# Order of the DMA transposes and of the loads of batches 3 and 4 in an attention and GEGLU kernel

## The chip, the cores and the metric

The kernel runs on one core of a Trainium2 chip. The metric is the device time of one execution in microseconds; of several runs the median is given. Beside it stands the profile of one execution: what each engine (TensorE or PE, VectorE or DVE, ScalarE or ACT, GpSimd or POOL, SyncE or SP) did, and what the DMA queues moved.

## The reference

Two steps follow each other: causal sliding-window attention with a linear bias by distance, for 8 batches, 8 heads, 576 positions and 64 dimensions per head, and then a gated feed-forward layer on its 4608 output rows of 512.

```python
scores = scale * np.matmul(q, k.transpose(0, 1, 3, 2))
rel = pos[:, None] - pos[None, :]
mask = (rel >= 0) & (rel < 128)
scores = np.where(mask, scores - slopes[h] * np.abs(rel), -1e9)
attn = softmax(scores)                       # over the keys
x = np.matmul(attn, v)                       # (8, 8, 576, 64) -> (4608, 512)
out = (gelu(x @ w_gate) * (x @ w_val)) @ w_out   # 512 -> 1536 -> 512
```

## The kernel before

Everything is scheduled by hand: the program text gives each engine's order of instructions, and each engine works through its own list.

**Two granularities run against each other.** The feed-forward part works on nine groups g of 512 tokens, the attention on eight batches b of 576 positions. The outer loop is over the groups. In group g, `gate_val` (L648 are its matmuls) makes the twelve hidden tiles `hT`, and then the products with `w_out` follow. Between these products the attention of the batches ahead is done: in group g the scores of batch b = g + 2, and the products of probabilities and values (`values`, matmuls at L502) of batch b - 1. From group 2 on, `out_products` does the output with seven block products instead of eight: `P(n, a)` is product n of half a, six matmuls at L749, and `O(what, a)` takes a result out of PSUM. Some of the factors are sums of blocks, kept in `left` (by group) and `right` (once).

**What the scores need.** `scores2(b, c)` (L301) multiplies transposed q with transposed k, two heads' pairs at a time. The transposes are made by DMA: `load_qk(b)` and `load_v(b)` request q, k and v from DRAM through POOL's queue (five requests each, line L115, with a cast from float32 to bfloat16) into `qs`, `ks` and `vb`, and `transposes_dma(b)` issues on SP's queue five transposes of q (L185, `qT<-qs`) and one large transpose of k (L178, `kT<-ks`). All five tensors have two buffers, taken by b % 2: batch 4 uses the buffers that batch 2 had.

**What sets the order on the queues.** SP's list holds the transposes, the stores of the output (`store`, L675) and short instructions that relay a matmul's end (L212). POOL's list holds the requests; a `tensor_copy` of two elements into `mark` is a way to wait: POOL reads one element of a tile and so stands until that tile has been written, and the requests behind it stand too. Group 1 has three such marks: on `ks[1]` (L1131, batch 3's k has been loaded), on `qT[1]` (L1132, its q has been transposed) and on `kT[1]` (L1134, its k has been transposed). v of batch 3 is requested behind the first two, q and k of batch 4 behind the third. In groups 2 to 5 a mark on a hidden tile (L1164) comes ahead of the next requests. `transposes_dma(g + 2)` is called at the top of group g, so the transposes of batch 4 are in SP's list ahead of all that group 2 stores.

**The softmax denominators.** From batch 3 on, `sums4` makes the row sums in the gate stage, `gather` (L451) writes their reciprocals to DRAM on ScalarE's queue and `spread_dma` (L457, `rb<-rd`) reads them back to all partitions, two transfers of 576 KB.

Of the kernel before, what the change touches and what calls it, by code (L numbers as in the profile page):

```python
# [34 lines left out]
def kernel(  # L35
# [10 lines left out]
    nc = tc.nc  # L46
# [27 lines left out]
    def keep_busy(ps, n, w=64, rhs=None):  # L74
        for _ in range(n):
# [21 lines left out]
    mark = consts.tile([1, 2], BF16, name="mark")  # L97

    qs, ks = ([consts.tile([128, 5, DM], BF16, name=f"{nm}s{i}") for i in range(2)]
              for nm in "qk")  # L100
    qT, kT = ([consts.tile([128, 4, 640], BF16, name=f"{nm}T{i}") for i in range(2)]
              for nm in "qk")
# [8 lines left out]
    def load(t, src, b, js=range(5), last=0):  # L111
        for j in js:
            n = rows(j)
            at = last if j == 4 else 0
            nc.gpsimd.dma_start(  # L115
                out=t[at:at + n, j, :].rearrange("p (h d) -> p h d", h=H),
                in_=src[b][:, 128 * j:128 * j + n, :].rearrange("h p d -> p h d"))

    def load_qk(b):
        load(qs[b % 2], q, b)  # L120
        load(ks[b % 2], k, b)

    def load_v(b, js=range(5)):
        load(vb[b % 2], v, b, js, 64)
# [44 lines left out]
    def transpose(b, what, c, copy):  # L169
        ps = bank().bitcast(BF16)  # L170
        for n, lo in ((0, 0), (1, 384)):
            transpose_runs(b, n, what, c, ps[:, lo:576])
        for n, lo in ((0, 0), (1, 384)):
            untangle(copy, b, n, what, c, c + 1, ps[:, lo:576])

    def transposes_dma(b):
        def of_k():
            nc.sync.dma_start_transpose(  # L178
                out=kT[b % 2].rearrange("p c (j t) -> p (c j) t", t=128),
                in_=ks[b % 2].rearrange("p j x -> p (j x)"))  # L180

        if b > 3:
            of_k()
        for j in range(5):
            nc.sync.dma_start_transpose(  # L185
                out=qT[b % 2][:, :, 128 * j:128 * j + 128], in_=qs[b % 2][:, j, :])
        if b <= 3:
            of_k()


# [482 lines left out]
    def store():  # L673
        for args in stores:
            nc.sync.dma_start(**args)  # L675
        stores.clear()
# [128 lines left out]
    for h in (0, 2, 4, 6):  # L805
        for w, src in ((0, q), (1, k)):
            (nc.scalar if w and h == 0 else nc.sync).dma_start(
                out=raw[w][h // 4].rearrange("p (h x) -> p h x", h=4)[:, h % 4:h % 4 + 2, :],
                in_=src[0][h:h + 2, 0:384, :].rearrange("h (p r) d -> p h (r d)", r=3))
# [115 lines left out]
    for do in inverse_a:  # L925
        do[1]()
    dve(out=pairs1.rearrange("p x (h d) -> p h x d", d=64),
        in_=vb[1].rearrange("p j x -> p (j x)")[:, 0:1536].rearrange(
            "p (h x d) -> p h x d", h=H, x=3))
# [46 lines left out]
    for n in range(4):  # L976
        nc.gpsimd.dma_start(
            out=wo[:, 3 * n:3 * n + 3, :],
            in_=moe_w_out[384 * n:384 * n + 384, :].rearrange("(c p) f -> p c f", p=128))
# [28 lines left out]
    def exp_table():  # L1008
        nc.scalar.preload_act_table_set("natural_log_exp_and_others")
# [4 lines left out]
    def out_products(g):  # L1014
        b = g + 2
        O = lambda what, a, copy=act: gather_out(g, a, what, copy)
        P = lambda n, a: product(g, n, a)
        if b > B:
            for n, after in ((1, ("p1",)), (2, ()), (6, ("u2", "c11")), (5, ("p5",)), (7, ("c22",)), (4, ("c21",)),
                             (3, ("c12",))):  # L1020
                for a in (0, 1):
                    P(n, a)
                    for what in after:
                        O(what, a)
                store()
            return
        P(1, 0)
        P(2, 0)
        O("p1", 0)
        urgent = 512 * (g + 2) - S * (b - 1)  # L1030
        if b == B:
            P(6, 0)
            O("u2", 0)
            O("c11", 0)
            P(5, 0)
            O("p5", 0)
            P(7, 0)
            O("c22", 0)
            scale = values(b - 1, later=True)
            P(4, 0)  # L1040
            O("c21", 0)
            P(3, 0)
            scale[0]()
            scale[1]()
            O("c12", 0)
            P(1, 1)
            O("p1", 1)
            store()
            P(2, 1)
            for do in scale[2:]:  # L1050
                do()
            O("c11", 1)
            P(6, 1)
            O("u2", 1)
            P(5, 1)
            O("p5", 1)
            P(7, 1)
            O("c22", 1)
            P(3, 1)
            O("c12", 1)  # L1060
            P(4, 1)
            O("c21", 1)
            return
        exp_table()
        O("c11", 0)
        if g == 2:
            P(6, 0)
        later = []
        scores2(b, 0, later)
        A = later[0]  # L1070
        if g > 2:
            P(6, 0)
        O("u2", 0, dve)
        P(5, 0)
        for n in (0, 1, 3):
            A[n]()
        O("p5", 0)
        A[2]()
        P(7, 0)
        O("c22", 0)  # L1080
        A[4]()
        for n in (5, 6, 7):
            A[n]()
        P(1, 1)
        P(4, 0)
        P(3, 0)
        O("p1", 1)
        O("c21", 0)
        O("c12", 0)
        A[8]()  # L1090
        A[9]()
        scores2(b, 2, later)
        A = later[1]
        P(2, 1)
        P(6, 1)
        O("u2", 1, dve)
        O("c11", 1)
        add(b, 0, None, (0,))
        P(5, 1)
        for n in (0, 1, 3, 5):  # L1100
            A[n]()
        O("p5", 1)
        A[2]()
        P(7, 1)
        O("c22", 1)
        A[4]()
        for n in (6, 7):
            A[n]()
        store()
        scale, more = values(b - 1, urgent=urgent)  # L1110
        for do in scale:
            do()
        P(4, 1)
        P(3, 1)
        O("c21", 1)
        for do in more:
            do()
        O("c12", 1)
        A[8]()
        A[9]()  # L1120
        add(b, 0, None, (2, 1))
        put_off.append(lambda: add(b, 2))
# [3 lines left out]
    for g in range(NG):  # L1126
        if 1 <= g < B - 2:
            transposes_dma(3 if g == 1 else g + 2)
        if g == 1:

            nc.gpsimd.tensor_copy(out=mark, in_=ks[1][0:1, 4, 0:2])  # L1131
            nc.gpsimd.tensor_copy(out=mark, in_=qT[1][0:1, 0, 512:514])  # L1132
            load_v(3)
            nc.gpsimd.tensor_copy(out=mark, in_=kT[1][0:1, 0, 512:514])  # L1134
            load_qk(4)
        for f in range(9 if g == 0 else 0, NF):
            gate_val(g, f)
            if f == 1:
                for do in put_off:
                    do()  # L1140
                put_off.clear()
                store()
            if g == 1 and f in (3, 5, 7, 9):
                combine_right(f // 2 - 1)
            if g in PRODUCTS and f in (7, 9, 11):
                combine_left(g, *{7: (0, 3), 9: (3, 5), 11: (5, 6)}[f])
            if g == 2 and f == 2:
                add(3, 2, act, (1,))
            if g == 0 and f == 10:
                masks_of_last_blocks(0, 8)  # L1150
            if g == 0 and f == 9:
                for c in range(4):
                    for w in (0, 1):
                        transpose(1, w, c, (act, dve)[w])
            if 2 <= g < B - 1:
                if f == (5 if g == 2 else 4):
                    sums4(g + 1)
                if f == (7 if g == 2 else 6):
                    gather(g + 1)
                if f == (9 if g == 2 else 8):  # L1160
                    spread_dma(g + 1)
                if f == 9 and g + 2 < B:

                    nc.gpsimd.tensor_copy(out=mark, in_=hid[g][0:1, f, 0:2])  # L1164
                    if g + 3 < B:
                        load_qk(g + 3)
                    load_v(g + 2)
        if g == 0:
            nc.gpsimd.memset(Ps[0][:, :, 0:64], 0.0)
            for t in (qs[1], ks[1]):  # L1170
                nc.gpsimd.memset(t[64:128, 4, :], 0.0)
        if g in PRODUCTS:
            out_products(g)
        else:
            for item in steps(g):
                if isinstance(item, int):
                    out_part(g, item)
                else:
                    RUN[item[0]](*item[1:])
            store()  # L1180
        if g == 0:
            load_v(2)
            nc.gpsimd.tensor_copy(out=mark, in_=qT[0][0:1, 0, 512:514])
            load_qk(3)
# [30 lines left out]
```

## Time and profile before

| | |
|---|---|
| time, median of 3 runs | 336.16 us (334.54 to 337.12) |
| profiled execution | 336.15 us, span 334.4 us from the first to the last instruction |
| granted TensorE clock | 0.999 |
| TensorE busy | 325.0 us, 97% |
| VectorE / ScalarE / GpSimd busy | 243.6 / 174.5 / 109.6 us |
| requests on POOL's queue (q0) | 107456 packets, 18.10 MB |
| stores and transposes on SP's queue (q1) | 38960 packets, 18.69 MB |

All times in the profile count from the span's start. A row of a timeline gives start, duration, engine, line, operation and tiles (written <- read), the number of merged instructions, and in brackets how long the engine had been idle and what released it. A row of SP ("SPq") or of ScalarE's queue ("ACTq") is the time in which the queue issues the transfer, not the transfer itself.

### The profile page before, as it was taken

The numbers are of one execution on the slowest core, as the hardware profiler recorded it, in microseconds if no ns is written. First come the engines' busy times: TensorE is split into PE (matmuls) and PEld (weight loads), VectorE is DVE, ScalarE is ACT, GpSimd is POOL, SyncE is SP. The second block draws the span as 40 slices with busy tenths as digits, with TensorE's granted clock in tenths as the row PEclk, the third lists the DMA queues.
The fourth block names the chain that finished last, engine by engine and source line by source line (L and its number), as shares of the span: only waits on it lengthen the run. The fifth ranks groups of instructions, "written<-read, shape, count | busy, mean of one in ns | idle before, by whom it ended". The sixth has DMA issues, their size and how long they took to land.

```text
span 334.4 us, 8797 instructions
## 1 busy us (share of the span) xinstructions
PE 325.0 (97%) x3544; PEld 192.8 (58%) x3544; DVE 243.6 (73%) x505; ACT 174.5 (52%) x341; POOL 109.6 (33%) x146
## 2 busy tenths in 40 slices
PE   8999999999999969999999999999999999999995
PEld 6566555444554448445854585448644864584474
DVE  7788776456779947978698969976998644833672
ACT  7974686437797346434843384239533233333331
POOL 6974788280582185005900490032000000000000
PEclk9999999999999999999999999999999999999999
DMA  8999999999999799949994799459204320012003
GB/s 213 169 197 190 205 165 181 136 214 127 133 218 114 143 186 189 150 113 176 181 159 128 150 174 194 128 131 135 77 1 106 77 92 0 2 45 83 0 0 126
DMA packets 149629, 43.53 MB, mean 130 GB/s; under 512 B 133556, under 2 KB 142420, under 8 KB 149588
## 3 DMA queue, kind: packets, MB, share of 16 engines
q0 software_dynamic: 107456, 18.10, 72.6%
q1 hardware_dynamic: 38960, 18.69, 25.5%
q10 hardware_dynamic: 3172, 6.19, 8.4%
q8 instruction: 27, 0.44, 0.5%
q14 instruction: 14, 0.11, 0.1%
HBM read 43.65 MB, written 9.53 MB: 159 GB/s over the span
## 4 chain that ended last, share of the span: by engine, by line
PE 84%; DVE 5%; ACT 4%; DMA 4%; issue 1%; DVEq 0%; ACTq 0%
PE ps L648 50%; PE ps L749 18%; PE ps L502 4%; PE ps L685 3%; ACT P L232 3%; DMA qT<-qs 2%; PE ps L301 2%; PE ps L219 2%; PE ps L705 2%; DMA out_dram<-osb 2%; DVE hT L656 2%; PE ps L76 1%; DVE P L235 1%; PE ps L438 1%; PE ps L157 1%
## 5 line engine op out<-in xcount | busy, mean ns | idle before, releaser
L655 ACT ACTIVATE gelu<-ps 128x512 bf16<-128x512 f32 (+3 forms) x117 | 65.6, 565 | 106.9 <-PE ps L648 99.3
L648 PE MATMUL ps<-xT,wg 128*128 128x512 bf16 (+4 forms) x472 | 112.8, 361 | 0.1
L648 PE MATMUL ps<-xT,wv 128*128 128x512 bf16 (+4 forms) x472 | 112.8, 361 | 0.0
L656 DVE TENSOR_TENSOR hT<-ps,gelu 128x512 bf16<-128x512 f32 (+3 forms) x117 | 73.3, 643 | 41.2 <-PE ps L648 35.6
L648 PEld LDWEIGHTS <-wv 128*128 128x128 bf16 x472 | 45.0, 98 | 48.8 <-DVE xT L556 0.5
L648 PEld LDWEIGHTS <-wg 128*128 128x128 bf16 x472 | 44.3, 98 | 46.7 <-issue 0.4
L232 ACT ACTIVATE P<-ps 128x512 bf16<-128x512 f32 (+1 forms) x108 | 52.4, 578 | 7.6 <-PE ps L301 5.5
L235 DVE TENSOR_TENSOR P<-P,emask 128x768 bf16<-128x768 bf16 x60 | 31.9, 554 | 12.0 <-ACT P L232 10.2
L749 PEld LDWEIGHTS <-hT 128*128 128x128 bf16 x336 | 32.0, 97 | 6.4
L115 POOL DMA_DIRECT2D vb<-in_v_dram x40 | 33.9, 883 | 4.8 <-DMA ks<-in_k_dram 2.0
L1164 POOL COPY mark<-hT 1x2 bf16<-1x2 bf16 x4 | 1.5, 366 | 79.5 <-DVE hT L656 79.5
L749 PEld LDWEIGHTS <-left 128*128 128x128 bf16 x252 | 24.3, 98 | 3.0
L115 POOL DMA_DIRECT2D ks<-in_k_dram x30 | 25.4, 893 | 1.2 <-DMA qs<-in_q_dram 1.1
L115 POOL DMA_DIRECT2D qs<-in_q_dram x30 | 25.1, 858 | 1.8 <-issue 0.9
L749 PE MATMUL ps<-right,hT 128*128 128x256 bf16 x168 | 22.1, 272 | 0.0
L749 PE MATMUL ps<-wo,hT 128*128 128x256 bf16 x168 | 21.0, 273 | 0.0
L749 PE MATMUL ps<-right,left 128*128 128x256 bf16 x168 | 20.5, 273 | 0.0
L502 PE MATMUL ps<-P,vb 64*64 64x192 bf16 (+2 forms) x752 | 18.3, 221 | 0.8 <-ACT P L232 0.7
L685 PE MATMUL ps<-wo,hT 128*128 128x512 bf16 x72 | 17.1, 380 | 0.2 <-issue 0.2
L502 PEld LDWEIGHTS <-vb 64*64 64x64 bf16 x752 | 15.0, 107 | 3.6 <-issue 2.7
L773 ACT COPY osb<-ps 128x256 f32<-128x256 f32 x14 | 5.6, 401 | 16.1 <-PE ps L749 16.1
L385 DVE TENSOR_TENSOR T<-P 64x1024 bf16<-64x1024 bf16 x20 | 13.7, 683 | 0.3
(113 smaller groups left out, 314.2 us busy)
## 6 DMA issues: line engine op xcount, KB each, us to landing
out_dram<-osb SPq DMA_DIRECT2D x36, 256.0 KB
rb<-rd ACTq DMA_DIRECT2D x10, 576.0 KB
vb<-in_v_dram POOLq DMA_DIRECT2D x32, 128.0 KB, 6.5
qs<-in_q_dram POOLq DMA_DIRECT2D x24, 128.0 KB, 6.0
ks<-in_k_dram POOLq DMA_DIRECT2D x24, 128.0 KB, 6.2
wo<-in_moe_w_out_dram POOLq DMA_DIRECT2D x4, 384.0 KB, 12.1
wg<-in_moe_w_gate_dram POOLq DMA_DIRECT2D x5, 256.0 KB, 7.1
wv<-in_moe_w_val_dram POOLq DMA_DIRECT2D x5, 256.0 KB, 8.9
```

The costliest lines, as they stand in the source:

```text
L115: nc.gpsimd.dma_start(out=t[at:at + n, j, :].rearrange("p (h d) -> p h d", h=H), in_=src[b][:, 128 * j:128 * j + n, :].rearrange("h p d -> ...
L219: nc.tensor.matmul(out=out, lhsT=keys(b, c, m)[half, :], rhs=qT[b % 2][half, c, q0:q0 + n], start=first, stop=True, skip_group_check=not f ...
L232: nc.scalar.activation(out=dst, in_=src, func=AF.Exp, scale=0.125)
L235: nc.vector.tensor_tensor(out=dst, in0=dst, in1=m, op=ALU.mult)
L301: mm = nc.tensor.matmul(out=ps[64 * x:64 * x + 64, col:col + w], lhsT=keys(b, c, m)[half, :], rhs=qT[b % 2][half, c, q0:q0 + w], start=Tru ...
L385: nc.vector.tensor_tensor(out=to[half, :, x:x + 7:2], in0=P[half, :, 0:10:3], in1=P[half, :, 1:11:3], op=ALU.add)
L502: mm = nc.tensor.matmul(out=out, lhsT=lhsT, rhs=prob(b)[half, c, i, col:col + q1 - q0], start=all(t[2] != u for t in todo[:n]), stop=True, ...
L648: nc.tensor.matmul(out=ps[:, a:e], lhsT=w[:, c, 128 * f:128 * (f + 1)], rhs=xT[:, c, t0 + lo + a:t0 + lo + e], start=begins and a == 0, st ...
L655: nc.scalar.activation(out=gl[:, 0:n], in_=pg, func=AF.Gelu)
L656: nc.vector.tensor_tensor(out=hid[g][:, f, lo:hi], in0=pv, in1=gl[:, 0:n], op=ALU.mult)
L685: nc.tensor.matmul(out=acc[g], lhsT=hid[g][:, f, 128 * t:128 * (t + 1)], rhs=wo[:, f, :], start=(f == 0), stop=(f == NF - 1))
L749: nc.tensor.matmul(out=made[g, a, into], lhsT=lhsT, rhs=rhs, start=first and i == 0, stop=i == NF // 2 - 1, skip_group_check=True)
```

## The change

Three things are changed. `transposes_dma` puts q's five transposes ahead of k's for batch 4 too, as it did for batches 2 and 3; for batches 5 and up k's stays first. In `out_products`, group 2 gets the order of the later groups: product P(6, 0) stands behind the first call of `scores2` instead of ahead of it. In group 1 the two marks on `ks[1]` and `qT[1]` go, and v of batch 3 is requested behind q and k of batch 4, so that all fifteen requests wait for the mark on `kT[1]` alone.

```diff
@@ transposes_dma
-        if b > 3:
+        if b > 4:
             of_k()
         for j in range(5):
             nc.sync.dma_start_transpose(
                 out=qT[b % 2][:, :, 128 * j:128 * j + 128], in_=qs[b % 2][:, j, :])
-        if b <= 3:
+        if b <= 4:
             of_k()
@@ out_products
         O("c11", 0)
-        if g == 2:
-            P(6, 0)
         later = []
         scores2(b, 0, later)
         A = later[0]
-        if g > 2:
-            P(6, 0)
+        P(6, 0)
         O("u2", 0, dve)
@@ the loop over the groups
         if g == 1:
 
-            nc.gpsimd.tensor_copy(out=mark, in_=ks[1][0:1, 4, 0:2])
-            nc.gpsimd.tensor_copy(out=mark, in_=qT[1][0:1, 0, 512:514])
-            load_v(3)
             nc.gpsimd.tensor_copy(out=mark, in_=kT[1][0:1, 0, 512:514])
             load_qk(4)
+            load_v(3)
```

## The prediction

> **What bounds the kernel now.** I read the page first, for the engine that is never idle.
>
> ```profile
> span 334.4 us, 8797 instructions
> ...
> PE 325.0 (97%) x3544; PEld 192.8 (58%) x3544; DVE 243.6 (73%) x505; ACT 174.5 (52%) x341; POOL 109.6 (33%) x146
> ```
>
> TensorE is busy for 325.0 of 334.4 us. So a change of DMA order can win only what TensorE idles. The view of waits names its one long wait on a transfer (columns: us in total, times, longest):
>
> ```profile
> PE ps L301 <- DMA qT<-qs: 2.8, 2, 2.7
> ```
>
> L301 is a score matmul, and the timeline of TensorE shows where it stands: in group 2, at the first scores of batch 4. The same stage of group 3, where nothing is late, follows.
>
> ```profile
> 118.26 1.47 PE L749 MATMUL ps<-wo,hT 128*128 128x256 bf16 x12
> 119.57 0.82 PE L749 MATMUL ps<-right,left 128*128 128x256 bf16 x6
> 120.57 0.28 PE L301 MATMUL ps<-qT,kT 64*64 64x64 bf16 x4 [0.18 <-DMA qT<-qs]
> 123.50 0.84 PE L301 MATMUL ps<-qT,kT 64*64 64x192 bf16 x40 [2.65 <-DMA qT<-qs]
> ...
> 134.50 1.03 PE L648 MATMUL ps<-xT,wg 128*128 128x512 bf16 x4
> ```
>
> ```profile
> 155.99 1.47 PE L749 MATMUL ps<-wo,hT 128*128 128x256 bf16 x12
> 157.39 0.87 PE L301 MATMUL ps<-qT,kT 64*64 64x64 bf16 x44
> ...
> 169.10 1.03 PE L648 MATMUL ps<-xT,wg 128*128 128x512 bf16 x4
> ```
>
> From the first product to the next group's first gate matmul, group 2 takes 134.50 - 118.26 = 16.24 us, and group 3 takes 169.10 - 155.99 = 13.11. The work is the same, so **3.13 us** is the full price of the late transposes, more than the 2.8 of the waits view, since the modelled ends of matmuls hide some idle time.
>
> Why are they late? The timelines of POOL's and of SP's queue:
>
> ```profile
> 69.66 4.33 POOL L115 DMA_DIRECT2D ks<-in_k_dram  x5
> 84.98 0.49 POOL L1131 COPY mark<-ks 1x2 bf16<-1x2 bf16 x1 [10.99 <-DMA ks<-in_k_dram]
> 85.55 0.17 POOL L1132 COPY mark<-qT 1x2 bf16<-1x2 bf16 x1
> 86.08 4.20 POOL L115 DMA_DIRECT2D vb<-in_v_dram  x5 [0.35 <-PE ps L502]
> 93.14 0.17 POOL L1134 COPY mark<-kT 1x2 bf16<-1x2 bf16 x1 [2.86 <-DMA kT<-ks]
> 93.65 4.20 POOL L115 DMA_DIRECT2D qs<-in_q_dram  x5 [0.34 <-issue]
> 97.79 4.24 POOL L115 DMA_DIRECT2D ks<-in_k_dram  x5
> 115.90 0.36 POOL L1164 COPY mark<-hT 1x2 bf16<-1x2 bf16 x1 [13.88 <-DVE hT L656]
> ```
>
> ```profile
> 71.90 7.70 SPq L185 DMA_TRANSPOSE qT<-qs  x5
> 85.04 3.08 SPq L178 DMA_TRANSPOSE kT<-ks  x1
> 88.22 9.29 SPq L675 DMA_DIRECT2D out_dram<-osb  x4
> 106.50 2.97 SPq L178 DMA_TRANSPOSE kT<-ks  x1
> 109.53 7.15 SPq L185 DMA_TRANSPOSE qT<-qs  x5
> ```
>
> Batch 4's q and k are requested only when batch 3's kT has landed (93.14), and that landing comes 8.1 us after its issue at 85.04, with v of batch 3 requested beside it at 86.08. SP then holds all of batch 4's transposes until k is there (106.50), though q was requested first, and it issues the last q transpose at the end of 109.53 to 116.68. There it meets another transfer, the spread of the sums' reciprocals over the partitions (L457). Here is the queue table in two windows, 86 to 89.5 and 116.2 to 121 us (columns: packets, MB, share of 16 engines), and then ScalarE's issues:
>
> ```profile
> q1 hardware_dynamic: 2494, 0.64, 98.3%
> q0 software_dynamic: 13, 0.00, 0.7%
> ```
>
> ```profile
> q10 hardware_dynamic: 479, 1.07, 98.8%
> q1 hardware_dynamic: 32, 0.00, 0.4%
> ```
>
> ```profile
> 110.75 1.72 ACTq L451 DMA_DIRECT2D rd<-r  x2
> ...
> 114.23 1.43 ACTq L457 DMA_DIRECT2D rb<-rd  x2
> ```
>
> q1 is SP's queue, q0 POOL's, q10 ScalarE's. While kT of batch 3 moved, the requested loads of v stood; while the spread moved, SP's transposes stood. So the last transpose of q, issued before the spread's data, lands after it, at 123.5.
>
> **The change part by part.** (1) The two marks at L1131 and L1132 go: 0.66 us of POOL, which then waits longer at the third mark. Nothing on the path.
>
> (2) v of batch 3 goes behind q and k of batch 4. Now kT of batch 3 has no loads beside it. It can't land before its last packet, 89.5, nor later than now, 93.1; I take 90.0, near the data, since nothing is queued behind it on POOL. The first q request follows its mark by 0.5 us (93.14 to 93.65): 90.5 instead of 93.65, **3.1 us earlier** (bounds 0 and 3.6). q is then requested from 90.5 to 94.7, k until 98.9, v until about 103.1, by the 4.2 us rows. v of batch 3 is read by values(3), which TensorE reaches only behind both score calls of batch 4, the first of them at about 119.6 (below); even the 11.0 us that the slowest loads took (below) has v there at 114, so its delay is hidden. The mark at 115.90 waits on DVE and stays.
>
> (3) q's five transposes go ahead of k's. SP is busy with stores until 97.5, which the change doesn't move, so they issue from 97.5; before, the last load of k landed 4.5 us after its request had been issued (102.03 to 106.50), and by that q is complete at about 99.2, before its last transpose is due. At 7.15 to 7.70 us for five they are issued by 105.2.
>
> (4) k's transpose now ends the sequence, and it needs k's loads, which now run beside q's transposes. Undisturbed that is the 4.5 us just used; beside q's transposes, in batch 3, 11.0 us (73.99 to 84.98). That is 103.4 or 109.9 here. Batch 3's transposes began in the middle of k's requests (71.90 in 69.66 to 73.99), here they begin in the last third (97.5 in 94.7 to 98.9) and behind a store, so I take the middle, 107. The transpose itself then needs between 4.5 us (85.04 to the last packet at 89.5) and the 8.1 us that it took beside v, which is again queued beside it. I take 8.1: **kT lands at 115**, with bounds 107.9 and 118.0.
>
> [...]
>
> (5) P(6,0) of group 2 moves behind the first scores, as in group 3 and later. So the scores are wanted after twelve product matmuls instead of eighteen: 118.26 + 1.31 = 119.57. That takes away 0.66 us of cover: were kT late, TensorE would idle that much longer before doing P(6,0). With kT at 115, and even at 118.0, there is no wait, and the stage takes the 13.11 us of group 3, which has this very order: **-3.13 us**.
>
> (6) The scores of batch 3 were held a little by kT as well:
>
> ```profile
> 90.81 2.12 PE L685 MATMUL ps<-wo,hT 128*128 128x512 bf16 x9
> 93.03 0.99 PE L301 MATMUL ps<-qT,kT 64*64 64x64 bf16 x44
> 93.96 2.12 PE L685 MATMUL ps<-wo,hT 128*128 128x512 bf16 x9
> 96.01 0.87 PE L301 MATMUL ps<-qT,kT 64*64 64x64 bf16 x44
> ```
>
> Nine L685 take 2.05 us (93.96 to 96.01), so the scores could begin at 92.86 instead of 93.03, and they took 0.12 longer than the next ones. With kT at 90 that is worth up to 0.29; I take **-0.2**.
>
> What is late next? In group 3 the first scores run at 157.39 without a wait, and the requests for their q and k hang on the mark at 115.90, which stays; being wanted 3.3 us earlier, they have the 38 us from 115.9 to 154.1. So I expect nothing in its place. Sum: 3.1 + 0.2 = 3.3 us. The profiled execution took 336.15 us (span 334.4 and 1.75 around it), the median is 336.16, so the result holds for both: **332.9 us**, 1.0% faster. One per cent (3.4 us) is about what a measurement of this kernel can tell from no change: the three times shown spread over 2.6 us. The forecast lies on that border.
>
> **The rivals.** (a) *The spread catches k's transpose* (chance 0.22). If k lands near 110 and kT's data runs to 115 or later, its completion falls between 116.2 and 121, where 32 packets of SP's queue moved. kT would land at 121 to 123.5. The stage then ends at 118.26 + 13.11 + (landing - 119.57), that is 132.8 to 135.3 against 134.50 now: from 1.7 us faster to 0.8 us slower, with (6) 334.3 to 336.8 us; middle 335.5. For it: the margin from 118.0 to 119.57 is thin, and q's last transpose met just this. Against it: the taken 115 lies ahead of the spread's data.
>
> (b) *k's transpose begins behind the spread* (0.06; the slower side). For batch 3 kT's packets moved from 86 on, 1 us behind the issue at 85.04. So from a landing of k at about 115 on, five later than the slowest row, no data passes before 116.2. The transfer then waits for 121 and runs beside batch 5's loads, requested behind the mark at 115.90; with the 8.1 us of kT beside loads it lands at 129, TensorE stands 9.5 us instead of 3.1, and the time is about 336.15 + 6.4 - 0.2 = 342.3 us. Against it: all rows of loads beside transposes end earlier.
>
> (c) *The gather is slowed instead* (0.10). The gather L451 at 110.75 and the spread behind it on ScalarE's queue now run beside kT and v, where before they ran beside q's transposes alone. ScalarE already waits for the gather in three groups, at most 1.2 us:
>
> ```profile
> ACT gelu L655 <- DMA rd<-r: 3.6, 3, 1.2
> ```
>
> A gather twice as slow would hold the last gelu tiles, and with them P(2,0), by one to two times those 1.2 us: 334 to 335 us.
>
> (d) *The order of q and k does nothing* (0.3, which lies inside the forecast's chance). By the sum, loads 3.1 us earlier alone would let kT issue at 103.4 and q until about 113.6, ahead of the spread. Then moving v is the cause and the swap and P(6,0) are idle. The time is that of the forecast; only an experiment tells them apart.
>
> **How the numbers follow.** The forecast, no wait left, has 0.62; (a) 0.22, (b) 0.06, (c) 0.10. Its own range is 331.8 to 334.0, 332.7 being the most that (5) and (6) can give (3.13 + 0.29) and about 1 us on either side for the spread of the times shown. The range starts there and reaches up into (a): 331.7 to 336.5. Faster by over 1% means below 332.8, a little under half of the forecast's 0.62: 0.30. Slower by over 1% is (b): 0.06. The rest, 0.64, is within 1%.
>
> **What would show it.** In the changed profile: the mark of kT at about 90 and q's requests right behind it; q's transposes at 97.5 and k's at about 107 on SP; on TensorE twelve L749, then 44 L301 without a gap, then twelve L749 of left and right factors; a stage of 13.1 us; no row of L301 waiting for qT or kT. The prediction is wrong in step (4) if k's transpose issues after 111 or if the wait stays under the name of kT; in step (2) if q's requests don't start before 92; in the idea that nothing is late next if the stage is 13.1 us and the span isn't 3 us shorter.

## The result, and the profile after

The changed kernel took 333.98 us (median of 22 executions, 332.81 to 336.93) beside 336.69 us (22 executions, 333.2 to 339.04) of the kernel before. The ratio is **0.9944, 95% interval 0.992 to 0.9968**: faster, by 0.6%. The difference of the medians is 2.7 us and the ratio says 1.9, because the ratio leaves out executions that lie over 1.5% above the fastest of their kernel: five of the kernel before, none of the changed one. The profiled execution took 332.81 us, 3.34 us less than the one of before.

The head of its page:

```profile
span 331.0 us, 8767 instructions
...
PE 321.9 (97%) x3513; PEld 192.7 (58%) x3544; DVE 244.2 (74%) x505; ACT 174.7 (53%) x341; POOL 109.5 (33%) x144
```

TensorE is still busy for 97%. Its timeline in group 2, the stage that took 16.24 us before:

```profile
118.02 1.47 PE L749 MATMUL ps<-wo,hT 128*128 128x256 bf16 x12
119.43 0.87 PE L301 MATMUL ps<-qT,kT 64*64 64x64 bf16 x44
120.23 1.48 PE L749 MATMUL ps<-right,left 128*128 128x256 bf16 x12
...
131.13 1.03 PE L648 MATMUL ps<-xT,wg 128*128 128x512 bf16 x4
```

Twelve products, 44 scores without a gap, twelve products; the bracket that named qT is gone, and the stage takes 131.13 - 118.02 = **13.11 us**. The requests on POOL's queue and the transposes on SP's (the lines of the file have moved: the mark on kT is L1128 here):

```profile
88.33 0.18 POOL L1128 COPY mark<-kT 1x2 bf16<-1x2 bf16 x1 [13.79 <-DMA kT<-ks]
88.85 4.20 POOL L115 DMA_DIRECT2D qs<-in_q_dram  x5 [0.35 <-issue]
93.01 4.23 POOL L115 DMA_DIRECT2D ks<-in_k_dram  x5
97.16 4.27 POOL L115 DMA_DIRECT2D vb<-in_v_dram  x5
```

```profile
83.23 3.12 SPq L178 DMA_TRANSPOSE kT<-ks  x1
86.45 10.58 SPq L675 DMA_DIRECT2D out_dram<-osb  x4
97.15 9.07 SPq L185 DMA_TRANSPOSE qT<-qs  x5
106.46 5.87 SPq L178 DMA_TRANSPOSE kT<-ks  x1
```

kT of batch 3 lands 5.1 us after its issue (83.23 to 88.33) instead of 8.1, q's transposes start behind the stores, and k's follows at 106.46. ScalarE's issues of the gather (L451) and the spread (L457):

```profile
110.51 1.72 ACTq L451 DMA_DIRECT2D rd<-r  x2
...
114.62 1.33 ACTq L457 DMA_DIRECT2D rb<-rd  x2
```

And the queue table while the spread moves, 116.2 to 121 us (columns: packets, MB, share of 16 engines):

```profile
q10 hardware_dynamic: 511, 1.13, 98.5%
q0 software_dynamic: 30, 0.00, 1.2%
```

SP's queue, q1, no longer has a row here: nothing of kT is left for the spread to catch. From group 3 on nothing differs between the two profiles: group 3's stage takes 13.11 us in both, and 13.10 or 13.11 in every other profile here. So the whole difference between them lies in group 2's stage (3.13 us) and a little ahead of it (0.24 us).

### The profile page after: what moved, and what is told of

It reads as the page before. It is cut to its first block, busy times and chain, and to the rows that moved or that the text cites. A ratio compares the mean times of both kernels' runs of the same rounds, so it can differ in the third digit from the quotient of the medians.

```text
span 331.0 us, 8767 instructions
## 1 busy us (share of the span) xinstructions
PE 321.9 (97%) x3513; PEld 192.7 (58%) x3544; DVE 244.2 (74%) x505; ACT 174.7 (53%) x341; POOL 109.5 (33%) x144
## 4 chain that ended last, share of the span: by engine, by line
PE 93%; ACT 2%; DMA 1%; issue 1%; DVE 1%; SPq 0%
PE ps L648 56%; PE ps L749 19%; PE ps L502 5%; PE ps L685 5%; PE ps L301 2%; ACT P L232 2%; PE ps L705 2%; PE ps L219 1%; DMA qs<-in_q_dram 1%; PE ps L438 1%; PE ps L157 1%; ACT osb L769 0%; SPq L807 0%; DVE qT L165 0%; ACT rb L599 0%
## 5 line engine op out<-in xcount | busy, mean ns | idle before, releaser
L648 PE MATMUL ps<-xT,wg 128*128 128x512 bf16 (+4 forms) x454 | 110.9, 360 | 1.1 <-issue 0.3
L502 PE MATMUL ps<-P,vb 64*64 64x192 bf16 (+2 forms) x752 | 18.5, 221 | 1.4 <-ACT P L232 0.7
L502 PEld LDWEIGHTS <-vb 64*64 64x64 bf16 x752 | 15.0, 107 | 4.3 <-issue 3.3
L685 PE MATMUL ps<-wo,hT 128*128 128x512 bf16 x66 | 15.9, 380 | 0.7 <-issue 0.6
```

What stands on the lines that cost most here:

```text
L502: mm = nc.tensor.matmul(out=out, lhsT=lhsT, rhs=prob(b)[half, c, i, col:col + q1 - q0], start=all(t[2] != u for t in todo[:n]), stop=True, ...
L648: nc.tensor.matmul(out=ps[:, a:e], lhsT=w[:, c, 128 * f:128 * (f + 1)], rhs=xT[:, c, t0 + lo + a:t0 + lo + e], start=begins and a == 0, st ...
L685: nc.tensor.matmul(out=acc[g], lhsT=hid[g][:, f, 128 * t:128 * (t + 1)], rhs=wo[:, f, :], start=(f == 0), stop=(f == NF - 1))
```

## The experiments

Four sets of kernels ran, each beside the kernel before: its medians were 338.08 (e1 to e4), 337.96 (e5 to e8), 337.9 (e9 to e11) and 338.7 us (e12 to e14). "The stage" is the time from group 2's first product to group 3's first gate matmul, as above.

**Which part does it? e1: v's move alone.**

```diff
-            nc.gpsimd.tensor_copy(out=mark, in_=ks[1][0:1, 4, 0:2])
-            nc.gpsimd.tensor_copy(out=mark, in_=qT[1][0:1, 0, 512:514])
-            load_v(3)
             nc.gpsimd.tensor_copy(out=mark, in_=kT[1][0:1, 0, 512:514])
             load_qk(4)
+            load_v(3)
```

> Only the requests move: v of batch 3 goes behind q and k of batch 4 and the two marks go, as in the changed kernel; k's transpose of batch 4 stays ahead of q's, and P(6,0) of group 2 stays ahead of the scores. Theory (what counts is when the last transpose lands against the spread's data from 116 on): q and k are requested at about 89, k lands at about 102.5, k's transpose issues at once and lands by about 110 beside v, and q's last transpose issues at 110 to 112 and lands at 113 to 116, so just ahead of the spread: the wait of group 2 is gone, the stage from the first L749 to the next L648 takes 13.1 to 13.5 us, and the time is that of the changed kernel within 0.3 us. Rival (the order of q and k is needed): q's last transpose is caught by the spread as before, lands at 121 to 123.5, the stage takes 15 to 16.5 us and the time is 2 to 3 us above the changed kernel.

Measured: 337.11 us (12 executions, 333.42 to 342.07), ratio 0.993 (0.9888 to 0.9972). The profiled execution took 342.07 us, the longest of them, and shows the old wait, longer: the stage takes 20.63 us. SP's queue, then TensorE:

```profile
106.29 3.84 SPq L178 DMA_TRANSPOSE kT<-ks  x1
110.19 8.91 SPq L185 DMA_TRANSPOSE qT<-qs  x5
```

```profile
124.05 0.37 PE L301 MATMUL ps<-qT,kT 64*64 64x64 bf16 x4 [3.85 <-DMA qT<-qs]
125.53 1.43 PE L301 MATMUL ps<-qT,kT 64*64 64x192 bf16 x40 [1.11 <-DMA qT<-qs]
```

With k's transpose first and v's loads beside the transposes, q's last is issued at 119.1, in the middle of the spread. So v's move alone does not cure the wait, against the expectation. Whether it helps a little stays open: its ratio's interval does not contain 1, the median is 1.0 us below that of the kernel before and 2.4 us above that of the changed kernel in the same set (e4, 334.69), and four of the twelve executions took under 335 us, beside one of 17 of the kernel before.

**e2: the order of q and k and P(6,0), with v's old place; e7: the order alone.** The edit of e7 is this; e2 has the move of P(6,0) as well.

```diff
-        if b > 3:
+        if b > 4:
             of_k()
...
-        if b <= 3:
+        if b <= 4:
             of_k()
```

> Only the order of the transposes and of P(6,0) changes, as in the changed kernel; v of batch 3 stays ahead of q and k of batch 4, with its marks. Theory: q and k are requested at 93.6 as before, q's transposes issue from 99 on, k lands between 107 and 111 beside them and its transpose, with no v behind it, needs 4.5 to 6 us: landing 112 to 117. If it is over before 116, the stage takes 13.1 us and the time is that of the changed kernel; if the spread catches it, it lands at 120 to 123.5 and the stage takes 14 to 17 us, with the price of P(6,0) on top. I lean to the first, at 113 to 115. Rival (the requests must move): the wait stays, now named for kT, and the time is within 1 us of the kernel before.

> The kernel before with q's transposes of batch 4 ahead of k's and nothing else: v stays in front, and P(6,0) of group 2 stays ahead of the scores. Theory (the order does it): k's transpose is one transfer that lands by 115 to 117, the wait is gone, the stage takes 13.1 to 13.3 us, and the time is that of the kernel with P(6,0) moved as well, 334.3 us or 0.9894 of before within 0.4%. Rival (P(6,0) matters): the time differs from that by over 1 us.

Measured: e2 334.33 us (6 executions), ratio 0.9894 (0.9864 to 0.9925); e7 333.86 us (9 executions), ratio 0.9926 (0.9887 to 0.9966). Their stages take 13.11 and 13.09 us. k's transpose comes later than in the changed kernel and is soon done (issued at 110.20 in e2, where no packet of SP's queue moved from 115 to 116); SP's queue of e7:

```profile
98.29 8.00 SPq L185 DMA_TRANSPOSE qT<-qs  x5
110.42 3.12 SPq L178 DMA_TRANSPOSE kT<-ks  x1
```

The two lines of order do what the whole change does; P(6,0) behind the scores adds nothing to see.

**What catches q's last transpose? e3: the kernel before, with only the spread called two gate tiles later.**

```diff
-                if f == (9 if g == 2 else 8):
+                if f == (11 if g == 2 else 8):
                     spread_dma(g + 1)
```

> The kernel before, with one thing changed: in group 2 the spread of the reciprocals (L457) is issued behind hidden tile 11 instead of tile 9, some 3.5 us later. Theory (the spread is what catches q's last transpose): q's last transpose lands at 117 to 118, ahead of the scores, the wait of 2.7 us is gone and the stage takes 13.1 to 13.5 us, so the time falls by about 3 us with nothing else moved; the reciprocals land at about 126 and are wanted at about 128. Rival (loads of batch 5 or the late requests as such hold the transposes): the wait stays above 2 us and the time stays that of the kernel before.

Measured: 333.92 us (6 executions), ratio 0.9881 (0.9854 to 0.9909), stage 13.09 us. SP's queue is as before, with q's last transpose issued by 116.8, and ScalarE issues the spread behind that, 4.2 us later than in the first profile of the kernel before:

```profile
109.65 7.13 SPq L185 DMA_TRANSPOSE qT<-qs  x5
```

```profile
118.47 1.33 ACTq L457 DMA_DIRECT2D rb<-rd  x2
```

No row of L301 waits for qT. The transposes were not too late for the scores; they were too late for the spread.

**How much does the kernel before lose? e5 and e6: the kernel before, two more profiles, no edit.**

> The kernel before, profiled once more. Theory: the wait of group 2 on q's transposes isn't a constant; it depends on how many of the five are caught by the spread, so the stage from the first L749 to the next L648 takes anything from 14 to 20 us here, and the time is about 333 us plus the stage's excess over 13.1 us, within 1 us. Rival: the stage takes 16.2 us as in the first profile, and what differs between executions of this kernel lies elsewhere.

> The kernel before, profiled a third time, for the same question. Theory: a stage that differs from the other two profiles by over 0.5 us, and a time that differs from theirs by the same amount within 1 us. Rival: the same stage, another time.

e5 took 334.3 us and e6 337.99. SP's queue and TensorE of e5:

```profile
108.55 7.05 SPq L185 DMA_TRANSPOSE qT<-qs  x5
```

```profile
118.51 1.47 PE L749 MATMUL ps<-wo,hT 128*128 128x256 bf16 x12
...
120.57 0.87 PE L301 MATMUL ps<-qT,kT 64*64 64x64 bf16 x44
...
131.60 1.03 PE L648 MATMUL ps<-xT,wg 128*128 128x512 bf16 x4
```

and of e6:

```profile
109.44 7.17 SPq L185 DMA_TRANSPOSE qT<-qs  x5
```

```profile
118.18 1.47 PE L749 MATMUL ps<-wo,hT 128*128 128x256 bf16 x12
...
120.69 0.28 PE L301 MATMUL ps<-qT,kT 64*64 64x64 bf16 x4 [0.38 <-DMA qT<-qs]
123.73 1.27 PE L301 MATMUL ps<-qT,kT 64*64 64x192 bf16 x40 [2.76 <-DMA qT<-qs]
124.93 1.46 PE L749 MATMUL ps<-right,left 128*128 128x256 bf16 x6
...
136.34 1.03 PE L648 MATMUL ps<-xT,wg 128*128 128x512 bf16 x4
```

The same program: in e5 q's last transpose is issued by 115.60, 1.1 us behind the start of the spread's issue (114.48), and the stage takes 13.09 us with no wait. In e6 it is issued by 116.61, 2.5 us behind it (114.15), the wait comes, and the stage takes 18.16. With 16.24 in the profile of the prediction, that is **0, 3.1 or 5.1 us of loss in three executions of one kernel**; 1.0 us in an issue lies between nothing and all. (e5 took 334.3 us, 1.3 more than its stage led me to expect: 2.8 us of it lie outside the span, against some 1.8 in e6 and in the first profile.) e6 loses more than its waits (3.14 us), and the rest lies where the granted clock was low: six products take 1.46 us instead of 0.82, and the windows of two microseconds (columns: span, busy time of PE, PEld, DVE, ACT and POOL, granted clock, DMA share, GB/s) show it at 0.50 and 0.65.

```profile
124.00:126.00 2.00, 2.00 (x43) 1.47 (x32) 0.56 (x1) 1.57 (x3) 1.39 (x2) 0.50 2.44 155
126.00:128.00 2.00, 2.00 (x14) 1.55 (x13) 0.31 (x1) 1.57 (x4) 1.80 (x3) 0.65 2.44 161
```

**Does the changed kernel stay at its best? e4, e9 and e12: the changed kernel again, no edit.**

> The changed kernel once more, on the chip of the other runs. Theory: a median 2.7 us below the kernel before (0.992), since the stage of group 2 lost 3.1 us in the profiles and the kernel before varies by more than that from run to run. Rival (the profile of the changed kernel was a lucky one): its profile here shows a wait of TensorE of 1 us or more on a transfer in group 2 or another stage, and the gain is near 1.9 us (0.9944).

> The changed kernel beside the kernel with the order of the transposes alone, on one chip. Theory: requesting v behind q and k of batch 4 does nothing for the wait, and costs a little where the gather has to wait behind k's transpose and v's loads (ScalarE then stands before the spread, as in the profile with the gate stage 0.5 us longer); so this median lies 0 to 0.8 us above that of the order alone. Rival: the earlier requests are worth something, and this median lies below it by 0.5 us or more.

> The changed kernel, beside the two below on one chip. Theory (what the moved transposes give is partly taken back where the gather L451 stands behind k's transpose and v's loads, so that ScalarE holds the last gelu tiles before it can issue the spread): median 334 to 335 us, slowest run over 336, and the spread's issue in the profile anywhere between 114.5 and 119. Rival (nothing is taken back, the profile with a stage of 16.8 us was a rare one): the median is that of the kernel with the late spread within 0.3 us.

Measured: 334.69, 334.89 and 333.51 us, ratios 0.9897 (0.987 to 0.9925), 0.9931 (0.9899 to 0.9964) and 0.9868 (0.9828 to 0.9908). The medians lie 3.4, 3.0 and 5.2 us below those of the kernel before in the same sets. The stages of the three profiles are 13.42, **16.83** and 13.32 us. e9 is the one to read. SP's queue, ScalarE and TensorE:

```profile
109.72 7.07 SPq L178 DMA_TRANSPOSE kT<-ks  x1
```

```profile
111.31 1.72 ACTq L451 DMA_DIRECT2D rd<-r  x2
...
118.67 1.33 ACTq L457 DMA_DIRECT2D rb<-rd  x2
120.11 1.09 ACT L655 ACTIVATE gelu<-ps 128x512 bf16<-128x512 f32 x2 [4.82 <-issue]
```

```profile
118.81 0.71 PE L749 MATMUL ps<-wo,hT 128*128 128x256 bf16 x5
121.49 0.94 PE L749 MATMUL ps<-wo,hT 128*128 128x256 bf16 x7 [1.97 <-DVE hT L656]
```

That is rival (c) of the prediction. The spread's issue stands on ScalarE until 118.67, and the gather that it reads moved its last five packets between 118 and 119; the last two gelu tiles stand behind it for 4.82 us, and the first product, P(1,0), stops after five of its six matmuls for want of a hidden tile (the rival had named the next product, P(2,0); the sixth matmul of P(1,0) already reads one of the last two tiles). The gather was issued at 111.31, in the middle of kT's transfer (109.72 on), and its packets moved with kT's last. Here is the queue table of e9 from 110 to 114 us:

```profile
q0 software_dynamic: 2341, 0.29, 124.0%
q1 hardware_dynamic: 994, 0.24, 65.0%
```

and from 117 to 119:

```profile
q1 hardware_dynamic: 1231, 0.31, 85.1%
q0 software_dynamic: 120, 0.02, 11.9%
q10 hardware_dynamic: 33, 0.02, 3.2%
```

In the first window POOL's loads (q0) take more of the time than kT (q1), and the gather (q10) has no row; 33 of its packets move in the second. In the first profile of the changed kernel the loads were nearly done by then, and from 110 to 114 us:

```profile
q1 hardware_dynamic: 3054, 0.77, 124.5%
q0 software_dynamic: 56, 0.01, 2.7%
q10 hardware_dynamic: 26, 0.01, 1.1%
```

What differs ahead of it is the mark on kT of batch 3: 88.33 there, 90.66 in e12, 91.86 in e4, 91.82 in e9, and the spread is issued at 114.62, 116.20, 116.76 and 118.67. e4 and e12 show rival (c) in small: ScalarE idles 2.99 and 2.89 us ahead of the last two gelu tiles, instead of some 1.1 where nothing holds them, and the first twelve product matmuls take 1.78 and 1.69 us instead of 1.47. With a later mark, v's loads run beside kT's transpose; but e4 and e9 have the same mark and their stages differ by 3.4 us (kT's transpose is issued at 108.34 in e4, at 109.72 in e9), so the mark is not all of it.

**Does rival (c) set the median? e8 and e13: the changed kernel with the spread late; e10: the order alone again; e11: the order alone with the spread late.** The edits are those of e3 and e7.

> The changed kernel with the spread of group 2 issued behind hidden tile 11 as well. Theory: nothing is left to win in group 2, since k's transpose lands ahead of the spread; the stage takes 13.1 us and the median is that of the changed kernel and of the kernel before with the late spread, 333.9 to 334.7 us. Rival (in some executions the spread still catches k's transpose in the changed kernel): the median falls 0.5 us or more below the changed kernel's and the slowest runs come closer.

> The changed kernel with the spread issued behind hidden tile 11, so that a late gather no longer holds any gelu tile of group 2. Theory: the stage takes 13.1 us in the profile, the median is 0.5 to 1.2 us below the changed kernel's, 333.3 to 333.9. Rival: no difference over 0.3 us.

> The kernel before with q's transposes of batch 4 ahead of k's and nothing else, beside the changed kernel. Theory: stage of group 2 at 13.1 us, median 333.5 to 334.2 us, at or below the changed kernel. Rival: above it by 0.5 us or more.

> Both remedies without the rest: the order of the transposes of batch 4 and the spread of group 2 issued behind hidden tile 11, v where it was. Theory: the wait is already gone by either, so the median is that of the order alone within 0.4 us; the stage takes 13.1 us. Rival: some executions of the order alone still hold ScalarE before the spread, and this median is lower by 0.5 us or more.

| | us (executions) | ratio | stage |
|---|---|---|---|
| e8 | 333.61 (12) | 0.9911 (0.9881 to 0.9941) | 13.11 |
| e13 | 333.54 (6) | 0.986 (0.9822 to 0.9898) | 13.67 |
| e10 | 334.46 (12) | 0.9923 (0.9891 to 0.9955) | 13.09 |
| e11 | 333.73 (6) | 0.9899 (0.9846 to 0.9952) | 13.42 |

With the spread late, no gelu tile stands behind the gather. What that is worth can't be told: of the two pairs that ran on one chip, one shows nothing (e13 333.54 beside e12 333.51, where I had expected 0.5 to 1.2 us, and 334 to 335 us for e12), the other 0.7 us (e11 333.73 beside e10 334.46), with intervals that overlap. The order alone and the whole change, side by side, differ as little: e10 334.46, e9 334.89. All executions together give 334.18 us for the changed kernel (46), 333.91 for the order alone (21) and 333.61 for every kernel with the late spread (30), beside 337.91 for the kernel before (93). They come from several sets, and the intervals of their ratios overlap: which version is best stays open. The late spread is the cheapest of them, one number, and its medians are no worse. It has a price of its own in two of its four profiles, e11 and e13: there TensorE stands 0.50 and 0.74 us at the products of probabilities and values (L502), and the profile names nothing that ends the wait. The late spread is issued at 117.31 and 117.08, instead of 114.62 in the first profile of the changed kernel; that the wait comes from this is not shown.

**e14: e2 once more.**

> The order of transposes and of P(6,0) as changed, v of batch 3 ahead as before. Theory: the gather waits less, since no loads of v run beside k's transpose; the spread issues at 115 to 116 and the median is 0 to 0.7 us below the changed kernel's. Rival (v's place doesn't matter for the gather): the same median within 0.3 us and a spread as late as in the changed kernel's profile.

Measured: 333.84 us (6 executions), ratio 0.9874 (0.9836 to 0.9912), stage 14.12 us. Its profile holds a small case of rival (a). SP's queue, ScalarE's, TensorE:

```profile
111.98 3.42 SPq L178 DMA_TRANSPOSE kT<-ks  x1
```

```profile
114.21 1.71 ACTq L457 DMA_DIRECT2D rb<-rd  x2
```

```profile
120.67 0.87 PE L301 MATMUL ps<-qT,kT 64*64 64x64 bf16 x44 [0.95 <-DMA kT<-ks]
```

k came 1.8 us later than in e2 (110.20). This time the gather (110.74) was ahead of kT, the spread went out at 114.21, ahead of the 115 to 116 that I had expected, and kT ended among its packets. So with v in its old place 1.8 us in k's loading lie between no wait and a small one. In the changed kernel k's transpose is issued earlier, at 106.46 to 109.72, but its issue takes longer, 5.87 to 7.07 us instead of the 3.19 and 3.42 of e2 and e14; that its margin is larger is not shown.

## Why the prediction was right and wrong

**Right: what the wait was and what takes it away.** It was a collision with the spread (e3), not transposes too late for the scores, and the order of q and k removes it (e7). Steps (3) and (4): forecast 97.5 and 107 for the two issues, measured 97.15 and 106.46, though q's five took 9.07 us to issue instead of 7.15 to 7.70. kT's landing has no row of its own; SP's queue moved 3054 packets from 110 to 114 us and none from 115 to 116, against a forecast of 115. In the other profiles of the changed kernel k's transpose is issued at 107.39 to 109.72, and kT's packets end by 117 (e4) and 119 (e9), the latter beyond the bound of 118.0. Step (5): no wait, 13.11 us, as worked out, in that profile. That it took 332.81 us against a forecast of 332.9 is luck: it is the shortest of 46 executions of the changed kernel.

**Right in form, other in size: step (2).** The requests were to come 3.1 us earlier. They came at 88.85 instead of 93.65, 4.8 us, since kT of batch 3 was issued earlier too, at 83.23. That was the exception. I took 5.0 us from kT's issue to the mark, without v's loads beside it; it measured 5.1 there, but 6.6 to 6.7 in five other profiles with v moved (e1, e4, e8, e9, e12), where the mark stands at 90.66 to 91.86 and q's requests start only 1.3 to 2.5 us earlier than 93.65. In e4 and e9 they start behind 92, which I had named as the sign that step (2) is wrong. With v in front the same time was 8.0 to 9.1 us in seven profiles (the first, e2, e3, e5, e6, e7, e14), so the place of v's requests accounts for a part of the 8.1; what holds kT for the rest is not shown. And 89.5 was not the time of kT's last packet, as steps (2) and (4) took it: from 89.5 to 93.2 another 111 packets of SP's queue under 512 bytes moved beside 2761 of v's loads, and with the 2494 before them they make 2605, against 2607 in the first profile of the changed kernel, which had all moved by 88.4.

**Rival (d) fell.** I gave it 0.3 that moving v is the cause and the order idle. The order alone takes the wait away (e7), and v's move alone does not (e1), though whether it does nothing is open. Its sum had k's transpose issue at 103.4 with the loads earlier; in e1 it was issued at 106.29, so the loads, asked for earlier, were hardly complete earlier (106.29 against 106.50), and the transposes, with v's loads behind k's, took 3.84 and 8.91 us to issue instead of 2.97 and 7.15. That v's loads did the latter is argued, not tested.

**Wrong: step (5)'s 3.13 us, taken as a constant of both kernels.** The sum promised 3.3 us; the first comparison gave 2.7 by the medians and 1.9 by the ratio. The sum was made on one execution and then carried to the median with "the result holds for both", because 336.15 and 336.16 agreed. What the runs showed in its place is a loss that differs from execution to execution, on either side. Before, the stage measured 13.09, 16.24 and 18.16 us. After, where I put 13.11 with no wait, it measured 13.11, 13.32, 13.42 and 16.83, the last by rival (c), to which I gave 0.10 and 1 to 2 us, and which cost 3.7 in e9 (1.97 of waiting, the rest while the granted clock was low). So 332.9 us is what the changed kernel does at its best (332.81 is the lowest of 46), not its median, which lies 1.1 us higher in the first comparison. I had 0.64 on a change within 1%, and 0.6% is that; but the interval, 0.992 to 0.9968, does not contain 1, so even 0.6% can be told from no change here, and the bound of 1% that I took for this was too coarse. In the experiments the changed kernel stood at 0.9868 to 0.9931, on both sides of the forecast 1.0%.

**Open.** How much of the 1.1 us is rival (c): e9 shows the mechanism in a profile, and e4 and e12 show it in small, but with it taken away the median did not move in the last set (e12 and e13, six executions each). A part lies ahead of group 2: its first product begins 0.25 to 0.79 us later in e4, e9 and e12 than in the first profile of the changed kernel, and what sets that is not shown.

**Step (6)** can't be seen: the first product of group 2 begins at 118.02 instead of 118.26, as forecast, but the changed kernel's own profiles have it at 118.02 to 118.81, and those of the kernel before at 118.18 to 118.51.

## What to carry to other kernels

When a transfer waits for another queue's transfer, ask how far apart they are: where a microsecond decides between all and nothing, one profile shows one draw, and two or three more of the *unchanged* kernel are the cheapest experiment there is. Move the transfer that collides before moving the ones that are hit: here one number (when the spread is called) took the wait away as the reordered transposes and requests did. And where an engine's queue issues a transfer that depends on a small one, as ScalarE's spread on the gather, count what stands behind that issue (in e9 two gelu tiles, for 4.82 us) before giving the small one a big neighbour.

## What the runs showed of the hardware

**Short idle times of TensorE were followed by a lower clock in some profiles and not in others.** In e6 two idle times of 0.38 and 2.76 us were followed by a granted clock of 0.50 and 0.65 in the next two windows; the stage lost 5.1 us, of which 3.1 were waits. In the profile of the prediction, 0.18 and 2.65 us were followed by 1.00:

```profile
124.00:126.00 2.00, 2.00 (x38) 1.74 (x29) 0.71 (x2) 2.00 (x5) 1.57 (x2) 1.00 2.42 154
```

In e9 one of 1.97 us was followed by this, a little over half the clock from 122 to 126:

```profile
122.00:124.00 2.00, 2.00 (x50) 1.60 (x49) 1.44 (x6) 1.97 (x4) 2.00 (x4) 0.60 1.18 221
124.00:126.00 2.00, 2.00 (x12) 1.45 (x11) 0.73 (x2) 1.07 (x3) 0.66 (x1) 0.54 1.55 201
```

So the length of the idle time alone, as the profile gives it with ends of matmuls that are modelled, does not decide: 1.97 us stood ahead of 0.60, and 2.65 ahead of 1.00. What else does is not shown.

**The few packets of one queue moved late beside another queue's big transfer.** The gather's 36 packets moved only as kT's ended (e9; in the first profile of the changed kernel 26 of them from 113 to 114 us, with kT's last 827), and beside the spread, in the profile of the prediction, 32 packets of SP's transposes moved in 4.8 us (in e1, in the same window, 512). Beside q's five transposes all 36 had moved by 114 in the first profile of the kernel before, and in its three profiles the spread behind the gather was issued at 114.15 to 114.48; in e14, where kT was issued 1.2 us behind the gather, they had moved by 114 as well. Whether the size of the one transfer or its place in time makes the gather late was not tried.
